# SwiGLU feed-forward: the first 512 tokens transposed on TensorE instead of by DMA

## The chip, the cores and the metric

The kernel runs on one core of a Trainium2 chip. The metric is the device time of one execution in microseconds (us), taken as the median over runs.

## The reference

With B, S, D, F = 1, 2048, 512, 1376 and everything in bf16, the function is a gated feed-forward layer:

```python
def reference(x, w_gate, w_up, w_down):
    g = _silu(x @ w_gate)
    u = x @ w_up
    return (g * u) @ w_down
```

x is [1, 2048, 512], w_gate and w_up are [512, 1376], w_down is [1376, 512].

## The kernel before, in words

Each engine has its own list of instructions, written out by hand; the lists meet only at semaphores. TensorE (PE) counts finished accumulation groups in s_P, ScalarE (ACT) counts its results in s_A, VectorE (DVE) in s_D, and each load has a semaphore of its own. What is in the order of a list is done in that order: a wait holds up everything behind it on that engine.

**Layout.** The contraction over D runs over the partitions, so x must lie in SBUF transposed: xT_sb is [128, 4, 2048], token along the free axis, and the four slices dk are the four blocks of 128 of D. TensorE computes gate and up with a 128x128 block of weights as the stationary operand and 512 tokens of xT_sb as the moving one.

**Stages.** The tokens go in four chunks c of 512 (SC). For each chunk PE works through ten feature tiles ft of 128, and for each tile one group G (gate) and one group U (up), both four matmuls of 512 columns (line 260), into one of eight PSUM banks in rotation. ACT applies silu to the G bank (line 215), DVE multiplies with the U bank and writes hT_sb in bf16 (line 222). The 96 features that are left are handled by a group X for each chunk (line 287) and by groups Y (line 298). Then sixteen groups O of eleven matmuls each (line 315) compute the output, DVE copies each bank to SBUF (line 226), and SyncE (SP) stores it (line 198).

**The start.** SP issues the loads one after the other: two transposing DMAs of 256 tokens each for the first chunk of x ("x0a" and "x0b", line 74), then the weight slabs of feature tiles 1, 2-3, 4-6 and 7-10 (line 79), three transposing DMAs for the other chunks of x, and w_down (lines 102 and 105). ACT issues the slab of feature tile 0 (wg0 and wu0) on its own queue, then loads its table with a dummy activation (line 204). GpSimd (POOL) sets four constants of one column each (the memsets, listed under line 338) and releases the barrier at which all engines start; it does nothing after that.

**PE before the data.** PE runs matmuls on a constant of ones into bank 7: nine of 512 columns (line 268) and three of 128 (line 271). Their results are not used. Then it does the first G and U in halves of 256 tokens, so that work can begin on x0a while x0b is on its way:

```python
            for n0, n1 in ((0, HT), (HT, SC)):
                for g in groups[0:2]:
                    gu_matmuls(g, n0, n1)
```

After that come all the other groups in the order of the plan, the first of which is called group 2 here (G of feature tile 1, over all 512 tokens of the first chunk). In front of a group stand waits for its load, for the readers of the group that had the same bank eight groups earlier, and, for O, for hT_sb.

Of the kernel before, what the change touches and what calls it, by code (L numbers as in the profile page):

```python
# [5 lines left out]
ALU = mybir.AluOpType  # L6
BF16 = mybir.dt.bfloat16
FP32 = mybir.dt.float32

N_WARM = 9  # L10
N_WARM_SHORT = 3


def bass_standalone__swiglu_ffn__prompt_kernel(nc, x, w_gate, w_up, w_down, out):
    _, S, D = x.shape
    F = w_gate.shape[1]
    P = 128
# [4 lines left out]
    SC = 512  # L22
# [2 lines left out]
    NST = S // P  # L25
    LASTA = 384
    HT = SC // 2
    NB = 8
    NSG = 4
    NOS = 3  # L30
# [2 lines left out]
    xf = x[0]  # L33
# [8 lines left out]
    with ExitStack() as es:  # L42
        sb = lambda name, shape, dt: es.enter_context(nc.sbuf_tensor(name, shape, dt))
        ps = lambda name, shape, dt: es.enter_context(nc.psum_tensor(name, shape, dt))
        sem = lambda name: es.enter_context(nc.semaphore(name))

        xT_sb = sb("xT_sb", [P, KD, S], BF16)
# [7 lines left out]
        o_sb = [sb(f"o_sb{i}", [P, D], BF16) for i in range(NOS)]  # L55
        banks = [ps(f"bank{i}", [P, 512], FP32) for i in range(NB)]

        s_P = sem("s_P")
        s_A = sem("s_A")
        s_D = sem("s_D")  # L60
# [3 lines left out]
        def load_sem(name):  # L64
            loads[name] = sem(f"s_{name}")
            return loads[name]

        ones_w = nc.const_aps.tensor(1.0, [P, P], BF16)
        ones_m = nc.const_aps.tensor(1.0, [P, SC], BF16)
# [3 lines left out]
        def load_x(eng, name, t0, t1):  # L73
            eng.dma_start_transpose(
                xT_sb[:, :, t0:t1], xf[t0:t1, :]
            ).then_inc(load_sem(name), 16)
# [15 lines left out]
            load_slab(act, *slabs[0])  # L92

        def loads_on_sync(sp):
            load_x(sp, "x0a", 0, HT)
            load_x(sp, "x0b", HT, SC)
            for a, b in slabs[1:]:
                load_slab(sp, a, b)
            load_w(sp, "wut", w_up, F - (F - 32), F - 32, F)
            for c in range(1, NSC):  # L100
                load_x(sp, f"x{c}", c * SC, (c + 1) * SC)
            sp.dma_start(
                wd_sb[:, 0:NFF, :], w_down[0:NFF * P, :].rearrange("(k p) d -> p k d", p=P)
            ).then_inc(load_sem("wd"), 16)
            sp.dma_start(wd_sb[0:F_LAST, NFF, :], w_down[NFF * P:F, :]).then_inc(load_sem("wdt"), 16)
# [3 lines left out]
        groups = []  # L109
# [3 lines left out]
        def add_group(kind, **what):  # L113
            g = dict(kind=kind, at=len(groups), bank=banks[len(groups) % NB], readers=[], **what)
            groups.append(g)
            return g

        def add_op(eng, g, **what):
            n_read[eng] += 1
            op = dict(g=g, at=n_read[eng], **what)  # L120
            (act_ops if eng == "A" else dve_ops).append(op)
            g["readers"].append((eng, op["at"]))
            return op

        sg_reader = []
        n_sg = 0
# [34 lines left out]
        def plan_y(pi):  # L161
            g = add_group("Y", pi=pi)
            for c in (2 * pi, 2 * pi + 1):
# [4 lines left out]
                )  # L168
                t_ready[c] = d["at"]

        for c in range(NSC):
            for ft in range(NFF):
                plan_pair(c, ft)
            plan_x(c)
# [4 lines left out]
        for t in range(NST):  # L179
            ob = t % NOS  # L180
            need = 16 * n_store[ob]
            halves = [(0, D)] if t < NST - 1 else [(0, LASTA), (LASTA, D)]
            for c0, c1 in halves:
                g = add_group("O", t=t, c0=c0, c1=c1)
# [9 lines left out]
        def on_sync(sp):  # L194
            loads_on_sync(sp)
            for t, c0, c1, ob, eng, n in stores:
                sp.wait_ge(s_A if eng == "A" else s_D, n)
                sp.dma_start(of[t * P:(t + 1) * P, c0:c1], o_sb[ob][:, c0:c1]).then_inc(s_out[ob], 16)
            for i in range(NOS):
                sp.wait_ge(s_out[i], 16 * n_store[i])  # L200

        def on_scalar(act):
            loads_on_scalar(act)
            act.activation(adummy[:, 0:4], zero_c, ACT.Silu)  # L204
            for op in act_ops:
                act.wait_ge(s_P, op["g"]["at"] + 1)
                if op["kind"] == "silu":
                    if op["free"]:
                        act.wait_ge(s_D, op["free"])
                    fn = ACT.Silu  # L210
                else:
                    if op["stored"][1]:
                        act.wait_ge(*op["stored"])
                    fn = ACT.Copy
                act.activation(op["out"], op["src"], fn).then_inc(s_A, 1)  # L215
# [13 lines left out]
        def on_tensor(pe):  # L229
            landed = set()  # L230

            def need(name):
                if name not in landed:
                    pe.wait_ge(loads[name], 16)
                    landed.add(name)

            read = {"A": 0, "D": 0}

            def after(eng, n):
                if n > read[eng]:  # L240
                    pe.wait_ge(s_A if eng == "A" else s_D, n)
                    read[eng] = n

            def free(g):
                if g["at"] >= NB:
                    for eng, n in groups[g["at"] - NB]["readers"]:
                        after(eng, n)

            def gu_matmuls(g, n0, n1):
                c, ft = g["c"], g["ft"]  # L250
                if c > 0:
                    need(f"x{c}")
                elif n0 < HT:
                    need("x0a")
                if c == 0 and n1 > HT:
                    need("x0b")
                need(("wg" if g["kind"] == "G" else "wu") + str(slab_of[ft]))
                col = (0 if g["kind"] == "G" else UPH) + ft * P
                for dk in range(KD):
                    ins = pe.matmul(  # L260
                        g["bank"][:, n0:n1], lhsT=w_sb[:, dk, col:col + P],
                        rhs=xT_sb[:, dk, c * SC + n0:c * SC + n1], start=(dk == 0), stop=(dk == KD - 1),
                    )
                if n1 == SC:
                    ins.then_inc(s_P, 1)

            for i in range(N_WARM):
                pe.matmul(banks[NB - 1][:, :], lhsT=ones_w, rhs=ones_m, start=True, stop=True)  # L268

            for i in range(N_WARM_SHORT):  # L270
                pe.matmul(banks[NB - 1][:, 0:P], lhsT=ones_w, rhs=ones_m[:, 0:P], start=True, stop=True)  # L271

            for n0, n1 in ((0, HT), (HT, SC)):
                for g in groups[0:2]:
                    gu_matmuls(g, n0, n1)

            for g in groups[2:]:
                free(g)
                kind = g["kind"]
                if kind in "GU":  # L280
                    gu_matmuls(g, 0, SC)
                elif kind == "X":
                    c = g["c"]
                    need(f"wg{slab_of[NFF]}")
                    need("wut")
                    for dk in range(KD):
                        ins = pe.matmul(  # L287
                            g["bank"][:, :], lhsT=w_sb[:, dk, XC0:XC0 + P],
                            rhs=xT_sb[:, dk, c * SC:(c + 1) * SC],
                            start=(dk == 0), stop=(dk == KD - 1),  # L290
                        )
                    ins.then_inc(s_P, 1)
                elif kind == "Y":
                    need(f"wu{slab_of[NFF]}")
                    for dk in range(KD):
                        for c in (2 * g["pi"], 2 * g["pi"] + 1):
                            y0, y1 = yblk(c)
                            ins = pe.matmul(  # L298
                                g["bank"][y0:y1, :], lhsT=w_sb[:, dk, YC0:YC0 + 64],
                                rhs=xT_sb[:, dk, c * SC:(c + 1) * SC],  # L300
                                start=(dk == 0), stop=(dk == KD - 1),
                                tile_position=(0, y0), skip_group_check=True,
                            )
                    ins.then_inc(s_P, 1)
                else:
                    t, c0, c1 = g["t"], g["c0"], g["c1"]
                    c = t // TPC
                    need("wd")
                    after("D", h_ready[c])
                    for fk in range(NFT):  # L310
                        K = P if fk < NFF else F_LAST
                        if fk == NFF:
                            need("wdt")
                            after("D", t_ready[c])
                        ins = pe.matmul(  # L315
                            g["bank"][:, 0:c1 - c0], lhsT=hT_sb[0:K, fk, t * P:(t + 1) * P],
                            rhs=wd_sb[0:K, fk, c0:c1], start=(fk == 0), stop=(fk == NFT - 1),
                        )
                    ins.then_inc(s_P, 1)

        on_sync(nc.sync)
        on_scalar(nc.scalar)
        on_tensor(nc.tensor)
        on_vector(nc.vector)
# [28 lines left out]
```

## Time and profile before

| what | value |
|---|---|
| median of 3 runs | 121.7 us (121.63 to 121.72) |
| the profiled execution, its time | 121.83 us |
| its span, first to last instruction of the program | 120.5 us |
| PE busy | 116.8 us (97% of the span) |
| DVE busy | 43.7 us (36%) |
| ACT busy | 30.3 us (25%) |
| POOL busy | 0.2 us, 4 instructions |
| granted TensorE clock, mean of the span | 1.0 |

Times in the profile count from the first instruction of the span. The chain is followed backwards from the last instruction, at each step to whatever released it. A matmul's own duration overlaps with the next one's, because matmuls are pipelined; what counts for PE is the spacing of their starts.

### The profile page before, as it was taken

How to read it: one execution, taken by the hardware profiler on the slowest of the kernel's cores; microseconds unless marked ns; L12 is line 12 of the kernel's file. 1: busy time of each engine (PE TensorE's matmuls, PEld its weight loads, DVE VectorE, ACT ScalarE, POOL GpSimd, SP SyncE). 2: the span in 40 equal slices, each digit the busy share in tenths (PEclk: the TensorE clock that was granted, in tenths of full speed). 3: DMA queues.
4: the chain of work that ended last, by engine and by line, in shares of the span. 5: the costliest groups of instructions: out<-in, count | busy, mean ns of one | idle time of the engine just before them, and what ended most of it. 6: DMA issues, size and time to landing. Idle time of an engine off the chain costs nothing.

```text
span 120.5 us, 1390 instructions
## 1 busy us (share of the span) xinstructions
PE 116.8 (97%) x549; PEld 53.9 (45%) x559; DVE 43.7 (36%) x64; ACT 30.3 (25%) x51; POOL 0.2 (0%) x4
## 2 busy tenths in 40 slices
PE   7899999999999999999999999999999999999993
PEld 2364444444444444444444444444444444444452
DVE  0024334444334444334444344467233223322420
ACT  4032333262332363332363332330000000000001
POOL 0000000000000000000000000000000000000000
DMA  4999999940000000000000000000211121112112
GB/s 79 227 301 375 284 234 145 322 139 0 0 0 0 0 0 5 0 0 3 3 0 0 0 5 0 0 0 0 87 44 44 45 91 44 44 60 71 44 44 87
DMA packets 18022, 8.51 MB, mean 71 GB/s; under 512 B 11520, under 2 KB 18016, under 8 KB 18016
## 3 DMA queue, kind: packets, MB, share of 16 engines
q1 hardware_dynamic: 16960, 8.16, 26.5%
q10 hardware_dynamic: 1056, 0.26, 1.0%
q8 instruction: 4, 0.07, 0.2%
q14 instruction: 2, 0.02, 0.0%
HBM read 4.23 MB, written 2.10 MB: 52 GB/s over the span
## 4 chain that ended last, share of the span: by engine, by line
PE 93%; DMA 4%; issue 1%; DVE 0%
PE bank L260 57%; PE bank L315 32%; DMA xT_sb<-in_x_dram 4%; PE bank L287 3%; PE bank L298 2%; DVE o_sb L226 0%
## 5 line engine op out<-in xcount | busy, mean ns | idle before, releaser
L260 PE MATMUL bank<-xT_sb,w_sb 128*128 128x512 bf16 (+1 forms) x321 | 69.5, 375 | 0.8 <-DMA xT_sb<-in_x_dram 0.5
L260 PEld LDWEIGHTS bank<-xT_sb,w_sb 128*128 128x128 bf16 x328 | 32.1, 98 | 37.7 <-DMA xT_sb<-in_x_dram 0.8
L222 DVE TENSOR_TENSOR hT_sb<-sg_sb,bank 128x512 bf16<-128x512 f32 x40 | 27.5, 688 | 46.3 <-PE bank L260 37.6
L315 PE MATMUL bank<-wd_sb,hT_sb 128*128 128x512 bf16 (+4 forms) x184 | 38.1, 366 | 0.2
L215 ACT ACTIVATE sg_sb<-bank 128x512 f32<-128x512 f32 x40 | 23.8, 596 | 43.6 <-PE bank L260 43.6
L315 PEld LDWEIGHTS bank<-wd_sb,hT_sb 128*128 128x128 bf16 (+1 forms) x187 | 17.8, 98 | 20.7 <-DVE hT_sb L222 0.4
L226 DVE CAST o_sb<-bank 128x512 bf16<-128x512 f32 (+1 forms) x16 | 10.7, 666 | 25.4 <-PE bank L315 25.3
L215 ACT ACTIVATE o_sb<-bank 128x384 bf16<-128x384 f32 x1 | 0.5, 490 | 38.2 <-PE bank L315 38.2
L268 PE MATMUL bank<-const-bfloat16-1.0 128*128 128x512 bf16 x9 | 4.0, 626 | 0.8 <-PEq L338 0.8
L287 PE MATMUL bank<-xT_sb,w_sb 128*128 128x512 bf16 x16 | 4.1, 379 | 0.1
L222 DVE TENSOR_TENSOR hT_sb<-sgx_sb,bank 32x512 bf16<-32x512 f32 x4 | 2.8, 692 | 3.5 <-ACT sgx_sb L215 3.5
L215 ACT ACTIVATE sgx_sb<-bank 32x512 f32<-32x512 f32 x4 | 2.3, 587 | 4.5 <-PE bank L287 4.5
L222 DVE TENSOR_TENSOR hT_sb<-sgy_sb,bank 64x512 bf16<-64x512 f32 x4 | 2.7, 684 | 0.1
L287 PEld LDWEIGHTS bank<-xT_sb,w_sb 128*128 128x128 bf16 x16 | 1.6, 98 | 1.9
L215 ACT ACTIVATE sgy_sb<-bank 64x512 f32<-64x512 f32 x4 | 2.4, 589 | 0.1
L268 PEld LDWEIGHTS bank<-const-bfloat16-1.0 128*128 128x128 bf16 x9 | 1.2, 138 | 2.7 <-issue 2.7
L298 PE MATMUL bank<-xT_sb,w_sb 128*64 128x512 bf16 x16 | 1.9, 382 | 0.0
L204 ACT ACT_TABLE_LOAD x1 | 1.3, 1283 | 1.8 <-issue 1.8
L298 PEld LDWEIGHTS bank<-xT_sb,w_sb 128*64 128x64 bf16 x16 | 0.8, 109 | 1.0 <-DVE hT_sb L222 0.4
L271 PEld LDWEIGHTS bank<-const-bfloat16-1.0 128*128 128x128 bf16 x3 | 0.4, 147 | 0.6 <-issue 0.6
L271 PE MATMUL bank<-const-bfloat16-1.0 128*128 128x128 bf16 x3 | 0.5, 311 | 0.0
L204 ACT ACTIVATE act_dummy<-const-float32-0.0 128x4 f32<-128x4 f32 x1 | 0.2, 205 | 0.0
(4 smaller groups left out, 0.4 us busy)
## 6 DMA issues: line engine op xcount, KB each, us to landing
out_dram<-o_sb SPq DMA_DIRECT2D x15, 128.0 KB, 1.7
wd_sb<-in_w_down_dram SPq DMA_DIRECT2D x1, 1280.0 KB, 6.5
w_sb<-in_w_gate_dram SPq DMA_DIRECT2D x1, 480.0 KB, 5.8
w_sb<-in_w_up_dram SPq DMA_DIRECT2D x1, 448.0 KB, 6.2
w_sb<-in_w_gate_dram SPq DMA_DIRECT2D x1, 384.0 KB, 4.5
w_sb<-in_w_up_dram SPq DMA_DIRECT2D x1, 384.0 KB, 5.0
w_sb<-in_w_gate_dram SPq DMA_DIRECT2D x1, 256.0 KB, 3.7
w_sb<-in_w_up_dram SPq DMA_DIRECT2D x1, 256.0 KB, 3.9
```

The costliest lines, as they stand in the source:

```text
L204: act.activation(adummy[:, 0:4], zero_c, ACT.Silu)
L215: act.activation(op["out"], op["src"], fn).then_inc(s_A, 1)
L222: ins = dve.tensor_tensor(op["out"], op["a"], op["b"], ALU.mult)
L226: ins = dve.tensor_copy(op["out"], op["src"])
L260: ins = pe.matmul(g["bank"][:, n0:n1], lhsT=w_sb[:, dk, col:col + P], rhs=xT_sb[:, dk, c * SC + n0:c * SC + n1], start=(dk == 0), stop=(dk ...
L268: pe.matmul(banks[NB - 1][:, :], lhsT=ones_w, rhs=ones_m, start=True, stop=True)
L271: pe.matmul(banks[NB - 1][:, 0:P], lhsT=ones_w, rhs=ones_m[:, 0:P], start=True, stop=True)
L287: ins = pe.matmul(g["bank"][:, :], lhsT=w_sb[:, dk, XC0:XC0 + P], rhs=xT_sb[:, dk, c * SC:(c + 1) * SC], start=(dk == 0), stop=(dk == KD - 1),
L298: ins = pe.matmul(g["bank"][y0:y1, :], lhsT=w_sb[:, dk, YC0:YC0 + 64], rhs=xT_sb[:, dk, c * SC:(c + 1) * SC], start=(dk == 0), stop=(dk == ...
L315: ins = pe.matmul(g["bank"][:, 0:c1 - c0], lhsT=hT_sb[0:K, fk, t * P:(t + 1) * P], rhs=wd_sb[0:K, fk, c0:c1], start=(fk == 0), stop=(fk == ...
```

## The change

The first chunk of x is no longer loaded by transposing DMAs. Four plain loads bring 128 tokens each into a new tile xn_sb, token on the partition. PE transposes each 128x128 block with a matmul against an identity matrix `ident`, two blocks to a half of a PSUM bank (viewed as bf16), and DVE and ACT copy the results to xT_sb: DVE the blocks dk 0 and 1, ACT the blocks dk 2 and 3, four copies of 128x2x128 each. They are put into the plan as eight groups T ahead of all others (NT = 8), so they use each of the eight banks once. `ident` is made by POOL from the constant of ones with one affine_select; s_I tells PE of it, and PE waits for s_I after its dummies and ahead of the first transpose. The dummies are four of 512 columns and three of 128. The first G and U are done in pieces of 128, 128 and 256 tokens, with the transposes of the token blocks 2 and 3 between the first and the second piece.

```diff
-N_WARM = 9
-N_WARM_SHORT = 3
+N_WARM = 4
+N_FILL = 3
...
         def loads_on_sync(sp):
-            load_x(sp, "x0a", 0, HT)
-            load_x(sp, "x0b", HT, SC)
+            for i in range(NXN):
+                sp.dma_start(xn_sb[:, i, :], xf[i * P:(i + 1) * P, :]).then_inc(load_sem(f"xn{i}"), 16)
...
+        def tview(bank):
+            return bank[:, 0:P].bitcast(BF16).rearrange("p (k t) -> p k t", k=2)
...
+        xt_ready = {}
+        for i in range(NXN):
+            for h, eng in enumerate("DA"):
+                g = add_group("T", i=i, h=h)
+                op = add_op(
+                    eng, g, kind="copy", out=xT_sb[:, 2 * h:2 * h + 2, i * P:(i + 1) * P],
+                    src=tview(g["bank"]), stored=(None, 0),
+                )
+                xt_ready[i, h] = (eng, op["at"])
+        NT = len(groups)
...
+        def on_gpsimd(pool):
+            pool.affine_select(
+                ident[:, :], ones_w, pattern=[[-1, P]], compare_op=ALU.is_equal, fill=0.0,
+                base=0, channel_multiplier=1,
+            ).then_inc(s_I, 1)
...
                 for dk in range(KD):
+                    if c == 0 and dk % 2 == 0:
+                        for i in range(n0 // P, min(n1 // P, NXN)):
+                            after(*xt_ready[i, dk // 2])
...
+            warm(N_WARM, SC)
+            pe.wait_ge(s_I, 1)
+            def transpose_x(i):
+                need(f"xn{i}")
+                for g in groups[2 * i:2 * i + 2]:
+                    for j in range(2):
+                        dk = 2 * g["h"] + j
+                        ins = pe.transpose(tview(g["bank"])[:, j, :], xn_sb[:, i, dk * P:(dk + 1) * P], ident[:, :])
+                    ins.then_inc(s_P, 1)
...
+            transpose_x(0)
+            transpose_x(1)
+            warm(N_FILL, P)
+            first_groups(0, P)
+            transpose_x(2)
+            transpose_x(3)
+            first_groups(P, 2 * P)
+            first_groups(HT, SC)
```

In the built program, POOL's list has one more instruction than the diff names: between the barrier and the affine_select stands an ISA instruction, listed under the line of the affine_select, that reloads POOL's library of routines (PseudoReloadLibraryIndex, index 0). The program before has none.

More of the change, by code (lines that the diff above doesn't have):

```diff
@@ L27, in bass_standalone__swiglu_ffn__prompt_kernel @@
     HT = SC // 2
+    NXN = SC // P
     NB = 8
@@ L56, in bass_standalone__swiglu_ffn__prompt_kernel @@
         banks = [ps(f"bank{i}", [P, 512], FP32) for i in range(NB)]
+        xn_sb = sb("xn_sb", [P, NXN, D], BF16)
+        ident = sb("ident", [P, P], BF16)
+        s_I = sem("s_I")
         s_P = sem("s_P")
@@ L252, in gu_matmuls @@
                     need(f"x{c}")
[L253 to L256, printed above, removed]
                 need(("wg" if g["kind"] == "G" else "wu") + str(slab_of[ft]))
@@ L265, in gu_matmuls, with warm, first_groups @@
                     ins.then_inc(s_P, 1)
[L267 to L274, printed above, removed]
-                    gu_matmuls(g, n0, n1)
-            for g in groups[2:]:
+            def warm(n, width):
+                for i in range(n):
+                    pe.matmul(banks[NB - 1][:, 0:width], lhsT=ones_w, rhs=ones_m[:, 0:width], start=True, stop=True)
+            warm(N_WARM, SC)
[7 more added lines that the diff above has]
+                    ins.then_inc(s_P, 1)
+            first = groups[NT:NT + 2]
+            def first_groups(n0, n1):
+                for g in first:
+                    free(g)
+                    gu_matmuls(g, n0, n1)
+            transpose_x(0)
[6 more added lines that the diff above has]
+            first_groups(HT, SC)
+            for g in groups[NT + 2:]:
                 free(g)
@@ L321, in bass_standalone__swiglu_ffn__prompt_kernel @@
         on_sync(nc.sync)
+        on_gpsimd(nc.gpsimd)
         on_scalar(nc.scalar)
```

## The prediction

> **What bounds the kernel now.** I read the chain first. After the first load it is PE alone, with steps of 0.05 us between its pieces:
>
> ```profile
> 0.73 4.81 DMA xT_sb<-in_x_dram
> 5.54 0.05 issue
> 5.59 6.72 PE bank L260 x37
> 12.32 0.05 issue
> 12.37 10.74 PE bank L260 x49
> ...
> 118.66 0.29 DVE o_sb L226
> ```
>
> So from 5.59 us on PE never waits for anything, and the change can only move the moment from which that holds. I measure it by the start of group 2, the first group of 512 columns, since everything behind it is the same in both kernels and runs at 0.22 us a matmul (10.74 / 49). Where is group 2? The windows by stretch, for line 260 alone (columns: stretch, its length, PE busy and count, PEld busy and count, granted clock, DMA share, GB/s):
>
> ```profile
> 5.59:6.20 0.61, 0.61 (x3) 0.43 (x4) 1.00 1.37 231
> 6.20:7.62 1.42, 1.42 (x14) 1.27 (x13) 1.00 1.14 292
> ```
>
> The sixteen matmuls of 256 columns end their issue at 7.62: three starts in the first 0.61 us (0.20 us each), thirteen in the next 1.42 (0.109 each; the fourteenth counted is the last of the row above, still running). So PE runs at half pace until about 6.2 us, though the granted clock says 1.00 in both. The dummies show the same half pace in the timeline, by the starts of their weight loads:
>
> ```profile
> 0.74 0.14 PEld L268 LDWEIGHTS bank<-const-bfloat16-1.0 128*128 128x128 bf16 x2 [0.74 <-issue]
> 1.15 0.15 PEld L268 LDWEIGHTS bank<-const-bfloat16-1.0 128*128 128x128 bf16 x1 [0.27 <-issue]
> 1.58 0.15 PEld L268 LDWEIGHTS bank<-const-bfloat16-1.0 128*128 128x128 bf16 x1 [0.28 <-issue]
> 2.00 0.15 PEld L268 LDWEIGHTS bank<-const-bfloat16-1.0 128*128 128x128 bf16 x1 [0.28 <-issue]
> ```
>
> 0.427 us for 512 columns is twice 0.22, and so 0.107 us for 128 columns and 0.213 for 256. The pace doubled 5.4 us after PE began (0.77 to 6.2), with one idle stretch of 0.5 us in between.
>
> Then POOL, since the change makes PE wait for it, and the two rows nearest to a reload of its library:
>
> ```profile
> PE 116.8 (97%) x549; PEld 53.9 (45%) x559; DVE 43.7 (36%) x64; ACT 30.3 (25%) x51; POOL 0.2 (0%) x4
> ...
> L204 ACT ACT_TABLE_LOAD x1 | 1.3, 1283 | 1.8 <-issue 1.8
> ```
>
> ```profile
> DMA to landing us min/median/max: 4.3/5.5/6.7
> ```
>
> The first says that POOL only sets constants; the program before never calls a routine of a library on it. The second is the one switch of tables that the profile shows, 1.28 us on ACT. The third is for the transposing loads of x: with the DMA engines full, a transfer takes up to 6.7 us from issue to landing.
>
> **The change, step by step.**
>
> *Loads.* Two transposing issues hold SP until 3.45 us, where the first weight slab is issued. Four plain ones cost between 0.33 us (SP's store of the same 128x512) and 0.53 us (ACT's wu0) each; at 0.4 the slabs and all behind them on SP (x1 to x3, w_down) are issued 1.1 us earlier. No wait before was for any of them, so this gains nothing. The x loads land between 0.73 + 1.7 = 2.4 us (a store's 1.7 us to landing) for the first and 1.9 + 4.1 = 6.0 us (the time of wu0) for the last.
>
> *The identity.* POOL is free at about 0.62 us, when it releases the barrier. Next on its list is the reload, then the affine_select, then s_I, for which PE waits with all transposes, and with them the copies, G, U and the whole kernel queued behind. The affine_select on 128 columns lies between a memset (0.10 us) and DVE's copy of 128x128 (0.29 us); I take 0.3. The reload has no row. If the library is found in place it costs next to nothing; an engine's own switch is 1.28 us; a fetch of code from memory while the loads fill the DMA engines is a transfer of the kind that took 6.7 us; at the far end it does not finish until the load stream does, 26 us in this trace. I take the fetch and the switch together, 6.7 + 1.3 = 8.0 us, because an explicit reload has to bring code in, and this one runs from 0.6 us on, in the middle of the load stream. Identity ready: 0.62 + 8.0 + 0.3 = 8.9 us. By then every x load and wg0 and wu0 (5.3 us at the latest before) have landed.
>
> *PE up to the identity.* Four dummies end their issue at 0.77 + 4 x 0.427 = 2.5 us. Then PE idles for 6.4 us. The pace had not risen by 2.5 us before either, so the first stage begins at half pace. Removing five dummies and changing the short ones is free: they ran in time spent waiting.
>
> *The first stage at half pace.* 16 transposes at 0.107 = 1.71; 3 dummies 0.32; 16 matmuls of 128 columns 1.71; 8 of 256 columns 1.71. Sum 5.45 us. It takes as long as the pace needed to double before (5.4 us), so I leave all of it at half pace. The copies lie beside it: DVE takes 0.29 us for 128x128 and 0.69 for 128x512, so about 0.42 for 256 columns; ACT 0.49 for 384 and 0.60 for 512, about 0.39. Block 0: two transposes issued by 0.21, finished at about 0.45, copied by DVE by 0.9 and by ACT by 1.1; the first G starts at 8 x 0.107 + 0.32 = 1.18. Blocks 2 and 3: the last copy ends about 0.6 us after its transposes and is covered by eight matmuls of 128 (0.86). At full pace that cover would be 0.44 us, and some 0.2 would show. Waiting ahead of ACT's silu and DVE's multiplication are only these copies, 1.7 us on each engine, in time that both spend idle.
>
> *Sum.* Group 2 starts at 8.9 + 5.45 = 14.4 us instead of 7.62: 6.8 us later. Nothing gives it back, since PE has no idle time after it. The profiled execution would go from 121.83 to 128.6; the median is 0.13 lower than that execution, so 128.5.
>
> [...]
>
> **The rivals.**
>
> *The identity is in time (faster).* If reload and affine_select together take under about 2 us, x leads. Then the transposes start at about 2.6 us, G and U at 3.8. The same 5.45 us at half pace, with the pace doubling at 6.2 as before, is 3.6 us of half-pace work by then and 1.85 / 2 = 0.9 us after: group 2 at about 7.1 to 7.3, so 0.3 to 0.5 us gained: 121.3. For it: POOL is otherwise empty, and a reload of what is in place could be short. The point from which it decides, by the same sum (6.2 + (T - 0.75) / 2 = 7.62): the identity, or x, at T = 3.6 us; each microsecond later costs half of one up to 6.2 us, and a whole one from there.
>
> *The identity is in time, but PE is too sparsely busy.* With five dummies of 512 less and gaps at 2.5 to 4.5 us for xn0, xn1, wg0 and wu0, the doubling may come 2 to 3 us later than 6.2. The whole first stage and a part of what follows then runs at half pace: group 2 at 8.3, and up to 1 us more: 122.3 to 123.5. The trace has only one idle stretch, 0.5 us, and cannot say.
>
> *The reload waits for the load stream.* The weights and x take the DMA engines until 26 us. If the reload takes 12 us or more, the time is 132.4 or more. Against it: ACT's queue was served between SP's loads (wg0 landed at 3.4 us, wu0 at 5.3).
>
> **How the numbers follow.** About 0.2% (0.25 us) is what a measurement of this kernel can tell from no change. Late identity, with a reload of 5 to 11 us: 0.80. All at half pace that gives 125.4 to 131.4 (each microsecond of the reload is one of the time), and a pace that doubles in the middle of the first stage takes up to 1.4 us off. This is the forecast, 128.5. Identity in time and faster: 0.07. Identity in time at a slow pace: 0.09, of which 0.03 ends within 0.2%. Later still: 0.04. So faster 0.07, same 0.03, slower 0.90. The two cases of an early identity and the last one stay outside the range (0.20), so it goes from 125.0 to 132.0, the ends of the forecast's own case.
>
> **What would show it.** Right: in the chain, a stretch of POOL (or of time put down to nothing) between 0.6 and about 9 us in place of the DMA; PE's idle time ahead of the transposes some 6 us, released by POOL; transposes and first matmuls spaced 0.107 us; SP's slabs issued from about 2.4 us; group 2 near 14.4; from there to the end the same 111 us as before. Wrong: the affine_select done before 3 us and the transposes released by a load. Then the identity step is wrong altogether, and the pace in the first stage decides the sign. If group 2 is late but the matmuls are spaced 0.056 us for 128 columns, only the pace is wrong.

## The result: slower by 0.9%, not by 5.6%

| | median | lowest to highest | runs |
|---|---|---|---|
| before | 121.47 us | 121.10 to 121.72 | 15 |
| changed | 122.30 us | 122.02 to 123.48 | 15 |

The ratio is 1.0092, 95% interval 1.0071 to 1.0112. The direction was forecast, the size was not: +0.83 us instead of +6.8, and the time lies below the stated range. Ratios here and below leave out an execution that took over 1.5% longer than the fastest of its kernel. The single times of the changed kernel spread over 1.46 us, those of before over 0.62. The profiled execution of the changed kernel took 122.02 us (span 120.8), the lower end of its own runs, and the profiled one of before, at 121.83 us, lies above all fifteen of its runs. So the two profiles differ by only 0.19 us and hide most of the loss; the rest has to come from experiments.

The chain of the changed kernel begins with x, not with POOL:

```profile
...
1.27 2.56 DMA xn_sb<-in_x_dram
3.83 0.05 issue
3.87 0.61 PE bank L302 x4
4.48 0.32 PE bank L293 x3
4.80 0.85 PE bank L284 x8
5.66 0.85 PE bank L302 x8
6.51 1.96 PE bank L284 x18
...
```

After block 1 has landed (3.83 us) PE never waits again. The timelines of POOL and PE show the step that failed, and how short the dummies are now:

```profile
0.89 0.29 POOL L222 TENSOR_SCALAR_AFFINE_SELECT ident<-const-bfloat16-1.0 128x128 bf16<-128x128 bf16 x1 [0.38 <-POOLq L383]
```

```profile
0.84 1.87 PE L293 MATMUL bank<-const-bfloat16-1.0 128*128 128x512 bf16 x4 [0.84 <-PEq L383]
3.17 1.32 PE L302 MATMUL bank<-ident,xn_sb 128*128 128x128 bf16 x8 [0.46 <-DMA xn_sb<-in_x_dram]
```

The affine_select starts at 0.89 us and takes 0.29 us (0.3 forecast). The trace has two MODIFY_POOL_CONFIG records ahead of it under its line, at 0.81 and 0.84 us, where before has none: the reload took less than 0.1 us. The identity is there at 1.2 us instead of 8.9, and the transposes are released by a load. The prediction named this as the sign that its identity step is wrong altogether.

Where is group 2? The windows of line 284, which is line 260 of before (columns as there):

```profile
4.59:6.83 2.24, 1.59 (x13) 1.43 (x14) 1.00 1.02 238
6.83:7.87 1.04, 1.04 (x13) 0.95 (x12) 1.00 1.08 312
```

The thirteen matmuls begun by 6.83 are spaced 0.107 us within their pieces (128 columns); after 6.83 the eight of 256 columns run at 0.109. So the pace doubled at 6.8 us and group 2 starts at 7.87, 0.25 us later than before (7.62). The prediction's own sum of the first stage fits with that start: from 3.17 to 6.83 there are 3.33 us of half-pace work (0.33 us were spent waiting for block 1), 2.12 of the 5.45 are left, at full pace 1.06: 7.89.

From group 2 on, nothing differs: the time of the profiled execution less the start of group 2 is between 114.1 and 114.3 us in both kernels and in all ten kernels of the experiments below (where the first record of group 2 is missing, its start is taken one spacing after the matmul ahead of it). So what a variant gains or loses, it gains or loses ahead of group 2, and a time less 114.15 gives an estimate of where group 2 began: 8.15 us for the median of the changed kernel, 9.3 for its slowest execution.

So x comes 2.4 us earlier (3.17 instead of 5.59), and the first stage is 2.7 us longer (4.70 instead of 2.03). Two theories for the 0.83 us of the median:

1. **Pace.** PE doubles its pace only after a stretch of nearly unbroken work. Four dummies end at 2.5 us, block 0 lands at 3.0 and block 1 at 3.8; the gaps put the doubling off, by a different amount in each execution. If the loads land as in this profile, the median's group 2 at 8.15 us stands for a doubling at about 7.4 us, an estimate.
2. **Work.** 16 transposes, 3 fills and narrower pieces are 2.0 us at half pace, 1.1 at full pace, that PE did not have before.

### The profile page after: what moved, and what is told of

Same layout as the page of the kernel before. It is cut to its first block, busy times and chain, and to the rows that moved or that the text cites. A ratio compares the mean times of both kernels' runs of the same rounds, so it can differ in the third digit from the quotient of the medians.

```text
span 120.8 us, 1444 instructions
## 1 busy us (share of the span) xinstructions
PE 116.9 (97%) x567; PEld 55.3 (46%) x578; DVE 44.9 (37%) x68; ACT 31.9 (26%) x55; POOL 0.5 (0%) x5
## 4 chain that ended last, share of the span: by engine, by line
PE 95%; DMA 2%; issue 1%; SPq 0%; DVE 0%
PE bank L284 57%; PE bank L359 31%; PE bank L331 3%; DMA xn_sb<-in_x_dram 2%; PE bank L342 2%; PE bank L302 1%; SPq L101 0%; PE bank L293 0%; DVE o_sb L251 0%
## 5 line engine op out<-in xcount | busy, mean ns | idle before, releaser
L284 PE MATMUL bank<-xT_sb,w_sb 128*128 128x512 bf16 (+2 forms) x329 | 70.3, 372 | 0.4
L284 PEld LDWEIGHTS bank<-xT_sb,w_sb 128*128 128x128 bf16 x336 | 32.9, 100 | 36.6
L359 PEld LDWEIGHTS bank<-wd_sb,hT_sb 128*128 128x128 bf16 (+1 forms) x187 | 17.8, 98 | 20.7 <-DVE hT_sb L247 0.4
L293 PE MATMUL bank<-const-bfloat16-1.0 128*128 128x512 bf16 (+1 forms) x7 | 2.4, 489 | 0.8 <-PEq L383 0.8
L251 DVE COPY xT_sb<-bank 128x256 bf16<-128x256 bf16 x4 | 1.2, 292 | 5.5 <-PE bank L302 5.3
L302 PE MATMUL bank<-ident,xn_sb 128*128 128x128 bf16 x16 | 2.3, 309 | 0.6 <-DMA xn_sb<-in_x_dram 0.5
L331 PEld LDWEIGHTS bank<-xT_sb,w_sb 128*128 128x128 bf16 x16 | 1.6, 98 | 1.9
L302 PEld LDWEIGHTS bank<-ident,xn_sb 128*128 128x128 bf16 x16 | 1.6, 140 | 1.7 <-issue 1.3
L240 ACT ACTIVATE xT_sb<-bank 128x256 bf16<-128x256 bf16 x4 | 1.5, 384 | 2.0 <-PE bank L302 2.0
L293 PEld LDWEIGHTS bank<-const-bfloat16-1.0 128*128 128x128 bf16 x7 | 0.8, 137 | 1.4 <-issue 1.4
```

The lines of the kernel that those rows point to most:

```text
L251: ins = dve.tensor_copy(op["out"], op["src"])
L284: ins = pe.matmul(g["bank"][:, n0:n1], lhsT=w_sb[:, dk, col:col + P], rhs=xT_sb[:, dk, c * SC + n0:c * SC + n1], start=(dk == 0), stop=(dk ...
L293: pe.matmul(banks[NB - 1][:, 0:width], lhsT=ones_w, rhs=ones_m[:, 0:width], start=True, stop=True)
L302: ins = pe.transpose(tview(g["bank"])[:, j, :], xn_sb[:, i, dk * P:(dk + 1) * P], ident[:, :])
L331: ins = pe.matmul(g["bank"][:, :], lhsT=w_sb[:, dk, XC0:XC0 + P], rhs=xT_sb[:, dk, c * SC:(c + 1) * SC], start=(dk == 0), stop=(dk == KD - 1),
L359: ins = pe.matmul(g["bank"][:, 0:c1 - c0], lhsT=hT_sb[0:K, fk, t * P:(t + 1) * P], rhs=wd_sb[0:K, fk, c0:c1], start=(fk == 0), stop=(fk == ...
```

## Experiments

### The dummies

Six instead of four in the changed kernel:

```diff
-N_WARM = 4
+N_WARM = 6
```

> The changed kernel with six instead of four dummies of 512 columns, so that PE works without a break until the first block of x is there (six dummies end at 0.84 + 6 x 0.427 = 3.4 us; xn0 landed at 3.03). Theory 1 (the pace: TensorE doubles its pace only after a stretch of nearly unbroken work, and the gaps at 2.5 to 3.2 and 3.6 to 3.9 us put that off): the pace doubles up to 1 us earlier in most executions, the median falls from 122.3 to 121.6 to 121.9 and the spread of the single times (1.46 us) falls below 0.8. Theory 2 (the work: 16 transposes and the narrow pieces are what costs): no gain, as x0's transposes only start 0.25 us later: 122.3 to 122.6, the spread as before.

Measured: 121.34 us median (121.10 to 122.14, 12 runs), ratio to before 0.9997, interval 0.9978 to 1.0016. Two more dummies take back the whole loss, although block 0's transposes now start later (3.39 us). Theory 2 falls as the cause of the loss. Theory 1 has the direction, but not the size: the median lies below its 121.6 to 121.9, and the spread is 1.04, wider than its 0.8. The profile does not show an earlier doubling, as the profiled execution was the longest of the twelve: its pace doubled at 6.85 us, as in the changed kernel's profile. By the sum used above, the median of 121.34 us stands for group 2 at 7.2 us and a doubling at about 5.2, an estimate, and the profiles of two other kernels that also begin with six dummies (below) have it at 5.1 and 6.5.

Four instead of nine in the kernel before:

```diff
-N_WARM = 9
+N_WARM = 4
```

> The kernel before with four instead of nine dummies of 512 columns (the three short ones stay), the one part of the change that removes PE work. PE then idles from about 2.8 to 5.6 us. Theory 1 (pace): the doubling waits for unbroken work that starts only at 5.6 us, so the whole first stage (3.5 us at half pace instead of 2.0) and some of what follows runs slow: 122.3 to 123.5, with a spread over 1 us. Theory 2 (work): the dummies are free, 121.3 to 121.7.

Measured: 123.23 us (122.79 to 124.03, 6 runs), ratio 1.0156, interval 1.0124 to 1.0188. The one part of the change that only removes PE work costs 1.8 us. Its windows show why: x was there earlier than before (5.37), but fifteen matmuls of 256 columns are spaced 0.213 us, and the doubling comes at 8.4:

```profile
5.37:8.33 2.96, 2.96 (x15) 2.09 (x15) 1.00 1.14 279
8.33:8.57 0.24, 0.24 (x3) 0.22 (x2) 1.00 1.13 383
```

None of the 512-column dummies in the changed kernel:

```diff
-N_WARM = 4
+N_WARM = 0
```

> The changed kernel with no dummies of 512 columns at all (the three fills stay), so that PE works only from the landing of xn0 on, 3.1 us. Theory 1 (pace): the pace doubles one window of nearly unbroken work after 3.9 us at the earliest, later than in the changed kernel in most executions: 122.6 to 123.6. Theory 2 (work): dummies only fill waiting time, and the time is that of the changed kernel, 122.0 to 122.5.

Measured: 123.26 us (122.39 to 123.41, 4 runs), ratio 1.0131, interval 1.0073 to 1.0190. In its profile the pace doubles at about 9.0 us. Zero, four, six dummies: 123.3, 122.3, 121.3 us (ratios to before 1.013, 1.009, 1.000). Theory 2 expected zero and four to be alike, and six to bring nothing.

### The work

Sixteen dummies in both kernels, so that the pace has doubled and nothing is waited for:

```diff
-N_WARM = 4
+N_WARM = 16
```

and in the kernel before

```diff
-N_WARM = 9
+N_WARM = 16
```

> The changed kernel with sixteen dummies, so that PE has doubled its pace and every load of the first stage has landed before the first transpose. With the next kernel (the kernel before with sixteen dummies) it measures what the transposes, fills and copies cost at full pace, with no wait for x in either. By the rows: 16 transposes at 0.056 us = 0.9, plus 0.1 to 0.3 for copies that are no longer covered: 1.0 to 1.2 us more than the kernel before with sixteen. Theory 2 has the same number here; theory 1 says that in the changed kernel itself the work costs up to twice that, because it runs at half pace.

> The kernel before with sixteen dummies, the partner of the last one. The dummies end at 0.8 + 16 x 0.427 = 7.6 us at half pace, at about 6 us if the pace doubles in the middle. The first matmul then starts at 6 to 7.6 us instead of 5.6, and the first stage takes 16 x 0.109 = 1.75 us: 121.6 to 123.2 us, with its spread from the moment of the doubling alone.

Measured: 124.26 us (123.47 to 124.37) and 122.42 us (121.95 to 123.19), 6 runs each. The medians differ by 1.84, more than the 1.0 to 1.2 expected, but with six runs they carry the luck of the doubling. The profiles measure the work itself; the windows from the end of the dummies of 512 columns to group 2, changed kernel first (columns: stretch, its length, busy time and count of PE, PEld, DVE, ACT and POOL, granted clock, DMA share, GB/s):

```profile
6.23:9.32 3.09, 3.09 (x44) 2.69 (x43) 1.03 (x4) 1.55 (x5) 0.00 (x0) 1.00 0.99 310
```

```profile
6.46:8.38 1.92, 1.92 (x20) 1.74 (x19) 0.00 (x0) 0.23 (x1) 0.00 (x0) 1.00 1.16 316
```

Both are at full pace, and both include three short dummies: 3.09 against 1.92 us, so the transposed start costs 1.17 us more. 16 x 0.056 = 0.90 is the transposes, the remaining 0.27 are copies without cover (six starts in the first and the third piece come 0.01 to 0.08 us late, 0.26 in all). Theory 2 is therefore true as a cost. In the changed kernel the cost is 2.0 us at half pace, and x comes 2.4 us earlier, so it was paid for by the earlier x; the kernel with six dummies, as fast as before, agrees with that.

Half of the transposes, with six dummies and no fills: blocks 0 and 1 by TensorE, tokens 256 to 511 by a transposing DMA. (The kernel that the expectation calls the one before it in the list is the next one below.)

```diff
-    NXN = SC // P
+    NXN = 2
...
+            load_x(sp, "x0b", HT, SC)
...
+                elif n1 > HT:
+                    need("x0b")
...
-            transpose_x(2)
-            transpose_x(3)
```

> As the kernel before it in this list (six dummies, no fills), but only the token blocks 0 and 1 come by plain loads and TensorE; tokens 256 to 511 come by one transposing DMA again, issued third on SP. Eight transposes and four copies fewer: theory 2 (work) gives 8 x 0.107 = 0.86 us less at half pace, 0.44 at full pace, if x0b lands by 6.0 us (in the kernel before the two transposing loads landed at 5.5 and 6.4): 120.4 to 120.9. If x0b lands later than PE needs it (about 6 us), the wait eats it up: 121.0 to 121.5.

Measured: 120.95 us (eleven runs from 120.69 to 121.39 and one of 123.17), ratio to before 0.9958, interval 0.9939 to 0.9976: faster than both kernels, and 0.05 us above what theory 2 expected. Its profiled execution took 120.78; its chain is PE alone from its first dummy on, up to and past group 2:

```profile
0.84 2.72 PE bank L296 x6
3.56 0.94 PE bank L305 x8
4.50 3.85 PE bank L287 x32
...
```

x0b landed at 5.46 us and the pieces of 256 columns began at 5.58, so the transposing DMA is in time by 0.1 us. Group 2 starts at 6.46. The pace doubled at 5.1 us here, and how much of the gain is that luck one profile cannot say. Behind group 2, at 8.2 us, PE waits 0.18 us for the weight slab of feature tiles 2 and 3, which was issued behind x0b and landed at 8.31.

The three fills alone, with all sixteen transposes and six dummies (the kernel to compare with is the one with six dummies above):

```diff
-N_FILL = 3
+N_FILL = 0
```

> The changed kernel with six dummies and without the three fills of 128 columns between the transposes of blocks 0 and 1 and the first G. The copies of block 0 should be done by then (DVE 0.29 us, ACT 0.38, both within the transposes of block 1), so no wait takes the place of the fills. Theory 2 (work): 3 x 0.107 = 0.32 us less at half pace, 0.17 at full pace: 121.0 to 121.2 against 121.34 with the fills. Theory 1 (pace) alone: no change, 121.3, as dummies only stand for work.

Measured: 121.69 us (120.93 to 122.15, 12 runs), ratio 1.0000, interval 0.9974 to 1.0027. The forecast gain did not show. The profile has a wait of 0.1 us for wu0 in the first U, which the fills had covered; the rest is within the spread of the doubling (6.5 us in its profile). This one is inconclusive.

### Do transposes count for the pace?

The kernel before, with eight of its nine dummies replaced (POOL makes the identity as in the changed kernel; that part of the diff is left out):

```diff
-            for i in range(N_WARM):
-                pe.matmul(banks[NB - 1][:, :], lhsT=ones_w, rhs=ones_m, start=True, stop=True)
+            pe.matmul(banks[NB - 1][:, :], lhsT=ones_w, rhs=ones_m, start=True, stop=True)
+            pe.wait_ge(s_I, 1)
+            for i in range(4 * (N_WARM - 1)):
+                pe.transpose(banks[NB - 1][:, 0:P // 2].bitcast(BF16), ones_w, ident[:, :])
```

> The kernel before with 32 transposes of 128 columns against an identity in place of eight of its nine dummies (the same 3.4 us of PE time, begun 0.4 us after the start when POOL has made the identity). It asks whether transposes count as work for the pace. If they do: as the kernel before, 121.1 to 121.7. If they do not: as the kernel before with four dummies or worse, 122.8 to 124.

Measured: 121.37 us (121.00 to 121.80, 12 runs), ratio 0.9992, interval 0.9973 to 1.0011. They count. In its profile the real matmuls run at full pace from the first one on (16 of 256 columns from 5.48 in 1.75 us):

```profile
5.47:7.23 1.76, 1.75 (x16) 1.56 (x17) 1.00 1.15 235
```

So the transposes of the changed kernel are not to blame for the late doubling. With the runs on the number of dummies, that leaves the idle time.

### The reload

The prediction's main term was 8 us for the reload. It took less than 0.1. Is a reload always short, or was the library in place? First a reload of another one:

```diff
         def on_gpsimd(pool):
+            pool.partition_broadcast(pool_dummy[:, 0:4], zero_c[0:1, :], channels=P)
```

> The changed kernel with a partition_broadcast of four columns on POOL ahead of the affine_select. It needs another library of POOL (index 1, which holds affine_select too), so the reload that stands ahead of it has to bring in another library than the one of index 0. Theory P (the term of 8 us was wrong because library 0 was in place already; a reload of another one costs what was forecast): the identity comes at 6 to 12 us, PE idles until then, and the time is 126 to 131 us. Theory Q (a reload is short whatever it names): the identity comes before 2.5 us, the time is that of the changed kernel, 122.0 to 123.5.

Measured: 122.59 us (121.99 to 123.32, 7 runs), ratio 1.0098, interval 1.0063 to 1.0133. That is the changed kernel's time. The built program has one reload, of index 1, ahead of the broadcast; the broadcast starts at 0.99 us and the affine_select follows at 1.13:

```profile
0.99 0.27 POOL L224 PARTITION_BROADCAST pool_dummy<-const-float32-0.0  x1 [0.50 <-POOLq L386]
1.13 0.37 POOL L225 TENSOR_SCALAR_AFFINE_SELECT ident<-const-bfloat16-1.0 128x128 bf16<-128x128 bf16 x1
```

Theory P as written fell. But if library 1 is still in place from the execution before, as theory P2 of the next run has it, this reload too named what was there, and a long reload of another library is still possible. The next kernel uses both libraries in each execution:

```diff
         def on_gpsimd(pool):
+            pool.partition_broadcast(pool_dummy[:, 0:4], zero_c[0:1, :], channels=P)
+            pool.iota(pool_count[:, 0:4], pattern=[[1, 4]], base=0, channel_multiplier=0)
```

> The changed kernel with two more instructions on POOL ahead of the affine_select: a partition_broadcast, which needs library 1, and then an iota, which needs library 0. So two reloads stand in POOL's list, one after the other and of different libraries, and at least one of them has to bring in what is not in place. Theory P2 (the one reload of each earlier kernel was short because its library was in place from the execution before): one of the two takes 6 us or more, the identity comes at 7 us or later, and the time is 126 us or more. Theory Q (a reload is short whatever it names): both take under 0.1 us, the identity comes before 3 us, and the time is that of the changed kernel, 122.0 to 123.5.

Measured: 136.27 us (two runs, 135.87 and 136.68), ratio 1.1219, interval 1.1155 to 1.1284. The built program has a reload of index 1 ahead of the broadcast (line 225) and one of index 0 ahead of the iota (line 226). The chain at its start:

```profile
...
1.07 0.01 POOLq L225
1.08 6.88 issue
7.96 0.28 POOL pool_dummy L225
8.24 0.07 POOLq L226 x2
8.32 9.10 issue
17.41 0.13 POOL pool_count L226
...
```

From each reload to the first instruction behind it pass 6.9 and 9.1 us, and the waits put the rest where the prediction had it:

```profile
PE bank L307 <- POOL ident L227: 15.2, 1, 15.2
```

Behind the same reload of library 1, the same broadcast starts at 0.99 us in the kernel that uses library 1 alone and at 7.96 us in this one, whose executions end with library 0. Theory P2 fits these runs: the two reloads that name another library than the one used last cost 6.9 and 9.1 us, and the one of the changed kernel, which names the library used last, under 0.1. What the 6.9 and 9.1 us are spent on, no row shows. In this kernel the identity is ready at 17.8 and group 2 starts at 22.5, 4.7 us later, with the pace doubling at 21.8.

## Why the prediction was wrong

**The step that failed: the identity at 8.9 us.** Its size is near that of the two long reloads: 8.0 us forecast, 6.9 and 9.1 measured. That it is made of a transfer (6.7 us) and a switch (1.3) was the author's estimate, and no run shows either in a reload. What failed is the choice "because an explicit reload has to bring code in": the reload took under 0.1 us. The prediction itself listed "if the library is found in place it costs next to nothing" as the lower bound and then gave the two cases of an early identity 0.16. Kernels are timed over repeated executions, and this kernel uses one library only. The other end of its bounds was the right one: the identity was ready at 0.89 + 0.29 = 1.18 us.

**The rival that came true** is the second: identity in time, PE too sparsely busy, 122.3 to 123.5 us. Measured 122.3, single times 122.02 to 123.48. It had a chance of 0.09. Its group 2 at 8.3 us and up to 1 us more fits with the 8.15 (median) to 9.3 us estimated above from the times; its doubling 2 to 3 us later than 6.2 is more than the profiled execution shows (6.8) or the median's estimate (7.4). That the forecast of slower came out right is luck: it rested on a late identity, and the loss comes from the pace.

**"Removing five dummies is free"** was wrong by the same mechanism. It was argued only from PE's time spent waiting; the kernel before with four dummies shows what they are worth, 1.8 us. In the changed kernel, two dummies are worth 1.0.

**Right:** the affine_select (0.29 against 0.3); the sum of the first stage (5.45 at half pace gives 7.89 against 7.87, once the measured wait and doubling are put in); SP's plain issues (one every 0.46 us against 0.4) and the slabs issued at 2.67 us against 2.4; no gain from that; x landing between 3.0 and 5.2 against 2.4 to 6.0. ACT's copies took 0.384 us (0.39 forecast). DVE's took 0.292, against 0.42 interpolated from rows with an fp32 source. A slip that decided nothing: the prediction lets its own case reach down to 125.4 less 1.4, that is 124.0 us, and yet begins the range at 125.0.

**The first rival** (121.3, x leads and the pace doubles as before) is what six dummies gave: 121.34. But that is no gain on before: at an unbroken start, the transposes eat what the earlier x brings. Only halving them leaves a net gain of 0.4%.

**What stays open.** When the pace doubles in a given execution was not predicted by any run. Work from 0.8 us on with gaps of 0.3 us at most had it double between 4.8 and 6.9 us in the profiles of the five kernels with six or sixteen dummies, and in the profile of before nine dummies had not doubled it by 4.88. What sets the moment no run shows, and that the spread of the times comes from it is only argued. How much idle time delays the doubling is open too: in the profile of before the pace doubled 0.6 us after an idle stretch of 0.5 us, and in the kernel before with four dummies 3.0 us after PE resumed work.

## What to carry to other kernels

Dummy matmuls that fill waiting time at the start are not free to remove: what counts here is that PE works with little or no break until the real matmuls (0.5 us idle in the kernel before did little harm, 2.4 us with four dummies cost 1.8), and the price of a later doubling is half of the time by which it is later (0.213 against 0.109 us for 256 columns). Price moved work at the pace that holds where it lands, and expect a spread from execution to execution (1.46 us over the fifteen runs of the changed kernel), so compare medians of a dozen runs and not two profiles. On POOL, ask which library was used last: with one library only, its reload took under 0.1 us in the changed kernel; with two in one execution, the reloads took 6.9 and 9.1 us. What a first execution pays was not measured.

## What the hardware showed unexpectedly

- The granted clock in the windows reads 1.00 while matmuls are spaced at half pace (0.213 us for 256 columns until 8.33 in the kernel before with four dummies, 0.109 after). The spacing of the starts is what shows the pace.
- Transposes raise the pace as matmuls do (121.37 us with 32 of them as dummies), and run at the full pace themselves (spaced 0.056 us in the changed kernel with sixteen dummies).
- DVE copies 128x256 bf16 out of PSUM in 0.292 us, about as long as 128x128 from fp32 (0.291).
